# Factors of batch 1 turned with batch 0's, three more stores on GpSimd, and the last chunk copied and stored in halves

## The chip, the cores and the metric

The kernel runs on one core of a Trainium2 chip. PE is TensorE (matrix products), DVE is VectorE, ACT is ScalarE, POOL is GpSimd, SP is SyncE, which only issues transfers. Each engine works through its own instructions in order and waits for the others by semaphores. The metric is the device time of one execution in microseconds; less is better.

## The reference

A chunked state space scan (4 batches, 8 heads, 768 steps, head width 32, state 16), and a GELU layer on its result:

```python
log_a = np.log(np.clip(a, 1e-06, 1.0))
for c in range(nc):                       # chunks of 32
    cum = np.cumsum(la, axis=-1)
    L = np.exp(cum[:, :, :, None] - cum[:, :, None, :]) * causal
    y_intra = einsum('bhij,bhjd->bhid', einsum('bhin,bhjn->bhij', Cc, Bc) * L, xc)
    y_inter = einsum('bhin,bhnd->bhid', Cc, state) * exp(cum)[..., None]
    y[:, :, sl] = y_intra + y_inter
    state = decay_full * state + sum_j(Bc x xc * decay_from_j)
x = y.transpose(0, 2, 1, 3).reshape(3072, 256)
out = gelu_tanh(x @ w_in) @ w_out         # 256 -> 2048 -> 256
```

## The kernel before

**Tiling.** The kernel uses chunks of 128 steps: 24 chunks `gc`, in 12 pairs `j` or `u` of 256 steps. Batch b holds pairs 3b to 3b+2, so pairs 0 to 2 are batch 0, and 3 to 5 batch 1. The first five pairs (`j < TOK`, TOK = 5) hold their steps in another order in memory, even and odd steps apart, than the later ones.

**Factors.** Decay is applied by scaling B with running products R of `a`, and C with 1/R. `f_clip` and `f_R` make R for all batches at once (`r_t`, 96 rows: part, batch, head). PE turns it so that steps lie on partitions: a product with `r_t` as the weights and the selection matrix `sel` as the moving operand, in fp32 (helper `rt_mm`, line 310). `f_RT` does this at the start for batch 0: two products of 24 columns, `rps[0]` in the PSUM bank pair `gb0`. DVE takes reciprocals (`f_rc0`, `f_rc1`), ACT copies R (`f_rlo`), and both stand in the tile `fac0`. `f_RTN` does it later, near 17 us: two products of 96 columns for all batches in the later order, and four of 8 columns for pairs 3 and 4, which have the earlier order. ACT copies this to `fac` (`f_rn`), and DVE takes reciprocals batch by batch (`f_pn`). `f_mul(j, i)` multiplies C (i = 1) or B (i = 0) of a pair with its factors.

**One pair.** After `f_mul`, B and C are transposed (on PE, `f_T`, for pairs 0 to 3, by a DMA issued on SP for later ones) and copied by ACT (`bt`). DVE masks heads (`f_F`, `ce`). PE then forms the Gram products `f_G` (L467 or L456, into `gb`), which DVE masks (`f_M`, tile `m`). `f_D` (L576 or L564) forms B times x for the state; DVE makes the running state from it (`f_S`, `s_new`; `f_SP`, `sp_new`). `f_Y` and `f_I` form y, and `xm` is its copy in bf16. x is cast to bf16 by GpSimd (`f_castx`).

**The layer.** For each pair, 32 matmuls `f_s1` (L642) fill four PSUM banks `bk` by turns, in eight groups of four, and ACT applies the GELU (`f_gelu`, tile `gT`, L650). Then 16 matmuls `f_s2` (L659) for each chunk; the result is copied out of PSUM (`f_oev`, tile `o_sb`; ACT, but DVE for chunks 21 and 23) and stored (`f_store`). Chunks 0 to 15 (`NPS = 16`) are stored by GpSimd's queue, and 16 to 23 by SP's. The pool of `o_sb` has six buffers.

**What sets the order.** The kernel builds a list of nodes with an engine, an estimated duration, dependencies and a priority. `run_order` plays them through, engine by engine, and the instructions are issued in the order that comes out; each engine then keeps that order. `FIRST` lists the first loads after `HEAD`, all issued on SP. The waits themselves are put in by the tile framework from what each instruction reads and writes.

Of the kernel before, what the change touches and what calls it, by code (L numbers as in the profile page):

```python
# [8 lines left out]
FP32 = mybir.dt.float32  # L9
# [104 lines left out]
def kernel(  # L114
# [10 lines left out]
    nc = tc.nc  # L125
# [3 lines left out]
    Q = 128  # L129
# [9 lines left out]
    TOK = 5  # L139
# [117 lines left out]
    pm = const.tile([128, 4 * D], BF16, name="pm")  # L257
    pp0 = const.tile([128, 4], FP32, name="pp0")
    r_t = const.tile([RA, W], FP32, name="r_t")
    fac0 = const.tile([128, 2, T3, 2, H], FP32, name="fac0")  # L260
    fac = const.tile([128, 2, batch, T3, 2, H], FP32, name="fac")
    pend = const.tile([128, NCH], FP32, name="pend")
    rps = {}
# [8 lines left out]

    X16 = {}
    state = {}
    gts, ops, hps = {}, {}, {}


    wo = moe_w_out.rearrange("(k f) m -> f k m", f=128)
# [32 lines left out]
                         start=True, stop=True, skip_group_check=True)  # L311

    def f_RT():
        rps[0] = GB[0][:, 0, 0:2 * T3 * H].rearrange("p (r t h) -> p t r h", r=2, t=T3)
        for r in range(2):
            rt_mm(GB[0][:, 0, r * T3 * H:(r + 1) * T3 * H],
                  r_t.rearrange("q (p r) -> q r p", r=2)[:, r], sel[:, :, 0:H])

    def f_RTN(bk):
        rps["n"] = bk[:, 0:NCH * H].rearrange("p (r i b h) -> p r b i h", r=2, i=T3, b=batch)  # L320
        for r in range(2):
            rt_mm(bk[:, r * RA:(r + 1) * RA], r_t[:, r * Q:(r + 1) * Q],
                  sel.rearrange("p i j -> p (i j)"))
        for j in range(T3, TOK):
            b, t = divmod(j, T3)
            for r in range(2):
                o = r * RA + (t * batch + b) * H
                rt_mm(bk[:, o:o + H], r_t.rearrange("q (p r) -> q r p", r=2)[:, r], sel[:, t, b * H:(b + 1) * H])

    def f_rc0():  # L330
        nc.vector.reciprocal(fac0[:, 1, 0], rps[0][:, 0])

    def f_rc1():
        nc.vector.reciprocal(fac0[:, 1, 1:T3], fac0[:, 0, 1:T3])

    def f_rlo():
        nc.scalar.activation(fac0[:, 0], rps[0], AF.Copy)

    def f_rn(r):
        nc.scalar.activation(fac[:, 0, :, :, r], rps["n"][:, r], AF.Copy)  # L340

    def f_pn(b):
        nc.vector.reciprocal(fac[:, 1, b], fac[:, 0, b])
# [36 lines left out]
    def f_mul(j, i):  # L380
        d = P[j]
        b, t = divmod(j, T3)
        if "bc16" not in d:
            d["bc16"] = work.tile([128, 2, 2, H, N], BF16, name="bc16")
        f = fac[:, i, b, t] if b else fac0[:, i, t]
        nc.vector.tensor_tensor(  # L386
            out=d["bc16"][:, i], in0=d["bc"][:, i].rearrange("p h (r n) -> p r h n", r=2) if j < TOK else
            d["bc"][:, i].rearrange("p h m -> p (h m)").rearrange("p (r h n) -> p r h n", r=2, h=H),
            in1=f.rearrange("p r (h o) -> p r h o", o=1).to_broadcast([128, 2, H, N]), op=ALU.mult)
# [264 lines left out]
    def f_s2(g, tt, q, bk=None):  # L654
# [3 lines left out]
        for fi in range(4 * q, 4 * q + 4):  # L658
            nc.tensor.matmul(out=ops[gc], lhsT=gts[g][:, fi, tt * Q:(tt + 1) * Q],  # L659
                             rhs=w_out_sb[:, fi, :], start=(fi == 0), stop=(fi == NF - 1),  # L660
                             skip_group_check=True)

    def f_oev(gc, eng):
        o_sb = opool.tile([128, d_model], FP32, name="o_sb")
        if eng == "ACT":
            nc.scalar.activation(o_sb, ops.pop(gc), AF.Copy)  # L666
        else:
            nc.vector.tensor_copy(out=o_sb, in_=ops.pop(gc))  # L668
        ops[gc] = o_sb
# [14 lines left out]
    DF = 1.0  # L684
    DW = 1.0
    LANES = 8
    FIRST = [("c", 3), ("b", 3), ("x", 3)]
    NPS = 16
    PET = {0: "ACT", 1: "ACT", 2: "ACT", 3: "ACT"}
    LB, LX, LI, LO, XD, XL = 0.92, 1.25, 1.42, 1.5, 0.6, 3.6  # L690
    HEAD = [("x", 0), ("x", 1), ("b", 1), ("wi", 1), ("wi", 2), ("wi", 3), ("b", 2), ("wo", 0), ("wo", 1), ("c", 2), ("wo", 2), ("wo", 3), ("x", 2)]
# [120 lines left out]
    frees(RTN, *rnn)  # L812
    pnn = {b: add("DVE", 0.42, f_pn, b, deps=rnn, prio=100 + b) for b in range(1, batch)}

    def gone(j):
        return [Yn.get(j - WB)]

    trn = add("POOL", 0.9, f_trk, deps=[wo_n[3][-1]], prio=25)
    for j in range(NP):
# [2 lines left out]
        b, t = divmod(j, T3)  # L822
        if b and t == 0:
            pnn[b].deps += Mn[j - (1 if j in PET else XA)]
        hold = Mn.get(j - (AHEAD if j in PET else XA), [])
        pj = PP if j == 1 else p
        ml = {i: shared(add("DVE", 0.43, f_mul, j, i, done=0.08, prio=pj - 0.1 * i if j else -179 - i,
                            deps=[bl[j, i], *hold, pnn[b] if b else rlo if not i else rc1 if j else rc0, *gone(j)]))
              for i in (1, 0)}
        bnn[j] = ml[0]  # L830
        if j == 1:
# [108 lines left out]
    for g, (c0, n) in enumerate(GROUPS):  # L940
        per = 512 // (n * Q)
        ends_ = []
        for tt in range(n):
            gc = c0 + tt
            if g < TWO and tt:
                prev = ahead
            ahead = list(prev)
            for q in range(4):
                need = [geln[(g, i)] for i in range(4 * n) if i * per <= 4 * q + 3]
                nd = add("PE", 0.437, f_s2, g, tt, q, deps=need[-1:] + wo_n[q] + prev,  # L950
                         prio=PB + 10 * c0 + 10 * n + 2.5 * ((tt + 2 * q) if g < TWO else 4 * tt + q) + 1.2,
                         alloc="bk" if q == 0 else ())
                if q == 0:
                    first = nd
                prev = [nd]
            ends_.append(nd)
            oeng = "DVE" if gc >= NCH - TAIL and gc % 2 else "ACT"
            oevn[gc] = add(oeng, 0.4, f_oev, gc, oeng, deps=[nd], prio=-40)
            frees(first, oevn[gc])
            if g < TWO:  # L960
                prev = list(ends_)
            if gc < NPS:
                st_n = add("POOL", 1.1, f_store, gc, nc.gpsimd, deps=[oevn[gc]], prio=2000)
            else:
                add("OUT", 0.05, f_store, gc, nc.sync, deps=[oevn[gc]], prio=gc)
# [65 lines left out]
```

## Time and profile before

| | us |
|---|---|
| median of 3 runs | 117.15 |
| the runs | 117.15, 116.15, 117.15 |
| the profiled execution's own time | 116.17 |
| its span | 114.5 |
| busy in it: PE / ACT / DVE / POOL | 107.7 / 72.8 / 59.6 / 30.1 |

The span is from the first to the last instruction that the profiler saw; the execution's own time also holds what lies around it. Busy times are summed for each engine over the span. Rows of the timeline begin with start and duration in us; `x4` is a count; in brackets stands the idle time of the engine just before, and what ended it. PE runs many matmuls overlapped, and PEld is its weight load. An fp32 product leaves two records.

### The profile page before, as it was taken

Reading aid. Unit: us, or ns where it says so; the run is one execution under the profiler, and the core shown is the slowest. Engines: PE = TensorE matmul, PEld = TensorE weight load, DVE = VectorE, ACT = ScalarE, POOL = GpSimd, SP = SyncE. Lnnn points to the kernel's source line nnn. Section 1 sums busy time; section 2 is a strip of 40 time slices with the busy share of each in tenths; the row PEclk is TensorE's granted clock in tenths of the full one; section 3 lists DMA queues with packets and bytes.
Section 4 is the critical chain, followed back from the end, with each engine's and each line's share of the span. In section 5 each row is a group of like instructions: output and inputs, shape, how many; then the busy total and the mean of one; then the engine's idle time right before and its main releaser. Section 6 shows DMA issues by size and latency. Waiting matters only on the chain.

```text
span 114.5 us, 3620 instructions
## 1 busy us (share of the span) xinstructions
PE 107.7 (94%) x1505; PEld 88.1 (77%) x1505; DVE 59.6 (52%) x133; ACT 72.8 (64%) x160; POOL 30.1 (26%) x57
## 2 busy tenths in 40 slices
PE   5987989999999999999999999999999999999970
PEld 2553669878878788887887887888878878878850
DVE  2799994069569293850952925907909227000110
ACT  0557685971469377686684793865966857949510
POOL 6834765746410421104211401412110000000000
PEclk9999999999999999999999999999999999999999
DMA  3999999999789897599977869674122011011021
GB/s 61 261 266 388 342 326 305 195 190 187 130 156 125 70 184 119 78 142 88 161 111 133 151 83 161 98 108 105 46 46 95 3 46 49 6 46 46 2 90 46
DMA packets 68880, 15.01 MB, mean 131 GB/s; under 512 B 64160, under 2 KB 67328, under 8 KB 68864
## 3 DMA queue, kind: packets, MB, share of 16 engines
q1 hardware_dynamic: 63888, 10.20, 53.3%
q10 hardware_dynamic: 4208, 2.49, 7.2%
q0 software_dynamic: 768, 2.10, 4.9%
q8 instruction: 11, 0.18, 0.7%
q14 instruction: 5, 0.04, 0.1%
HBM read 10.58 MB, written 3.15 MB: 120 GB/s over the span
## 4 chain that ended last, share of the span: by engine, by line
PE 85%; DVE 6%; ACT 4%; issue 2%; DVEq 0%
PE bk L659 37%; PE bk L642 33%; PE gb L993 4%; PE bk L526 2%; DVE sp_new L625 2%; PE gb L456 1%; ACT gT L650 1%; PE bk L310 1%; PE bk L500 1%; ACT bt L287 1%; DVE ce L432 1%; PE bk L549 1%; PE gb L467 1%; ACT sp_new L620 1%; PE gb L310 1%
## 5 line engine op out<-in xcount | busy, mean ns | idle before, releaser
L650 ACT ACTIVATE gT<-bk 128x512 bf16<-128x512 f32 x96 | 50.3, 604 | 7.6 <-PE bk L642 7.4
L659 PE MATMUL bk<-w_out_sb,gT 128*128 128x256 bf16 x384 | 48.7, 273 | 0.0
L642 PE MATMUL bk<-xm,w_in_sb 128*128 128x256 bf16 x384 | 47.2, 273 | 0.3 <-DVE s_new L609 0.3
L659 PEld LDWEIGHTS <-gT 128*128 128x128 bf16 x384 | 36.6, 98 | 6.1 <-issue 1.8
L642 PEld LDWEIGHTS <-w_in_sb 128*128 128x128 bf16 x384 | 37.3, 98 | 5.1 <-issue 0.6
L674 POOL DMA_DIRECT2D out_dram<-o_sb x16 | 8.9, 554 | 44.0 <-ACT o_sb L666 42.0
L477 DVE TENSOR_TENSOR m<-gb,trk 128x1024 bf16<-128x1024 f32 x14 | 17.0, 1216 | 0.0
L666 ACT ACTIVATE o_sb<-bk 128x256 f32<-128x256 f32 x22 | 8.5, 386 | 12.1 <-PE bk L659 6.0
L609 DVE SCALAR_TENSOR_TENSOR s_new<-s_new,pend,bk 128x64 f32<-128x64 f32 x16 | 4.4, 274 | 18.8 <-ACT xm L287 18.7
L287 ACT ACTIVATE xm<-bk 128x256 bf16<-128x256 f32 x22 | 7.4, 381 | 9.2 <-PE bk L500 6.9
L386 DVE TENSOR_TENSOR bc<-bc,fac 128x256 bf16<-128x256 f32 x24 | 10.9, 480 | 1.1 <-DMA bc<-in_C_dram 1.0
L477 DVE TENSOR_TENSOR m<-gb,tri 128x1024 bf16<-128x1024 f32 x8 | 9.6, 1216 | 0.2 <-PE gb L467 0.2
L289 POOL CAST x<-x_t 128x512 bf16<-128x512 f32 x12 | 7.5, 628 | 5.8 <-DMA x_t<-in_x_dram 5.7
L432 DVE TENSOR_SCALAR ce<-bt,par 128x256 bf16<-128x256 bf16 x22 | 5.6, 294 | 5.8 <-ACT bt L287 5.7
L625 DVE SCALAR_TENSOR_TENSOR sp_new<-s_new,pend,pm 128x128 bf16<-128x128 f32 x19 | 8.3, 464 | 0.0
L668 DVE COPY o_sb<-bk 128x256 f32<-128x256 f32 x2 | 0.8, 424 | 14.0 <-PE bk L659 14.0
L993 PE MATMUL gb<-wz 128*128 128x512 bf16 (+2 forms) x17 | 5.7, 465 | 1.3 <-DVE warm L221 1.3
L993 PEld LDWEIGHTS <-wz 128*128 128x128 bf16 x25 | 2.9, 127 | 3.9 <-issue 2.2
L607 DVE COPY s_new<-bk 128x64 f32<-128x64 f32 x3 | 0.7, 225 | 8.5 <-ACT xm L287 7.7
L289 POOL CAST w_in_sb<-wf 128x1024 bf16<-128x1024 f32 x4 | 4.6, 1157 | 1.6 <-DMA wf<-in_moe_w_in_dram 1.6
L289 POOL CAST w_out_sb<-wf 128x1024 bf16<-128x1024 f32 (+1 forms) x4 | 3.8, 940 | 2.5 <-DMA wf<-in_moe_w_out_dram 2.5
L456 PE MATMUL gb<-ce,bt 32*64 32x256 bf16 x112 | 3.3, 274 | 0.0
(78 smaller groups left out, 58.4 us busy)
## 6 DMA issues: line engine op xcount, KB each, us to landing
wf<-in_moe_w_in_dram ACTq DMA_DIRECT2D x4, 512.0 KB, 7.8
wf<-in_moe_w_out_dram SPq DMA_DIRECT2D x4, 512.0 KB, 6.7
out_dram<-o_sb POOLq DMA_DIRECT2D x16, 128.0 KB, 2.7
x_t<-in_x_dram SPq DMA_DIRECT2D x14, 128.0 KB, 3.3
x_t<-in_x_dram SPq DMA_DIRECT2D x5, 256.0 KB, 5.7
out_dram<-o_sb SPq DMA_DIRECT2D x8, 128.0 KB, 1.7
bc<-in_C_dram SPq DMA_DIRECT2D x14, 64.0 KB, 3.4
bc<-in_B_dram SPq DMA_DIRECT2D x14, 64.0 KB, 3.4
```

The lines of the kernel that those rows point to most:

```text
L287: nc.scalar.activation(o, i, AF.Copy)
L289: nc.gpsimd.tensor_copy(out=o, in_=i)
L386: nc.vector.tensor_tensor(out=d["bc16"][:, i], in0=d["bc"][:, i].rearrange("p h (r n) -> p r h n", r=2) if j < TOK else d["bc"][:, i].rear ...
L432: nc.vector.tensor_scalar(out=d["ce"][:, e], in0=v, scalar1=par[:, e:e + 1], scalar2=None, op0=ALU.mult)
L477: nc.vector.tensor_tensor(out=state[("m", u, f)].rearrange("p g r e t -> p g (r e t)"), in0=state.pop(("gc", u, f), gram[f]).rearrange("p ...
L625: nc.vector.scalar_tensor_tensor(out=sp_new.rearrange("p (j d) -> p j d", j=2), in0=state[("s", gc)].rearrange("p (o d) -> p o d", o=1).to ...
L642: nc.tensor.matmul(out=hp[:, j * nt:(j + 1) * nt], lhsT=w_in_sb[:, kc, fi * 128:(fi + 1) * 128], rhs=xm[:, kc, c0 * Q:c0 * Q + nt], start= ...
L650: nc.scalar.activation(gts[g][:, i * per:(i + 1) * per, 0:nt], hps.pop((g, i)).rearrange("p (j t) -> p j t", j=per), AF.Gelu_apprx_tanh)
L659: nc.tensor.matmul(out=ops[gc], lhsT=gts[g][:, fi, tt * Q:(tt + 1) * Q], rhs=w_out_sb[:, fi, :], start=(fi == 0), stop=(fi == NF - 1), ski ...
L666: nc.scalar.activation(o_sb, ops.pop(gc), AF.Copy)
L674: q.dma_start(out=o.rearrange("(p r) m -> r p m", r=2)[r] if u < TOK else o[r * Q:(r + 1) * Q], in_=ops.pop(gc))
L993: nc.tensor.matmul(out=bank[:, 0:128 * w], lhsT=wz[:, 0:128], rhs=wz[:, 0:128 * w], start=True, stop=True)
```

## The change

Four things are changed.

- `f_RT` takes 16 columns of `sel` for each part instead of 8, so 48 columns in each product instead of 24: batches 0 and 1. `fac0` becomes twice as wide. The reciprocals of batch 0 and the copy on ACT go with it, and a new node `f_p3` on DVE takes the reciprocals of batch 1 for pairs 3 and 4. `f_RTN` loses its four 8-column products. `f_mul` takes the factors of all pairs below TOK from `fac0`.
- `FIRST` has another order of loads (C of pair 4 ahead of x of pair 3).
- `NPS` is 19 instead of 16: chunks 16 to 18 are stored by GpSimd's queue.
- The last chunk's output is copied in two halves of 128 columns, one on ACT and one on DVE, and each half is stored by a queue of its own, ACT's and SP's.

```diff
-    fac0 = const.tile([128, 2, T3, 2, H], FP32, name="fac0")
+    fac0 = const.tile([128, 2, T3, 2, 2 * H], FP32, name="fac0")
...
     def f_RT():
-        rps[0] = GB[0][:, 0, 0:2 * T3 * H].rearrange("p (r t h) -> p t r h", r=2, t=T3)
+        n = T3 * 2 * H
+        rps[0] = GB[0][:, 0, 0:2 * n].rearrange("p (r t c) -> p t r c", r=2, t=T3)
         for r in range(2):
-            rt_mm(GB[0][:, 0, r * T3 * H:(r + 1) * T3 * H],
-                  r_t.rearrange("q (p r) -> q r p", r=2)[:, r], sel[:, :, 0:H])
+            rt_mm(GB[0][:, 0, r * n:(r + 1) * n], r_t.rearrange("q (p r) -> q r p", r=2)[:, r], sel[:, :, 0:2 * H])
...
-        for j in range(T3, TOK):
-            b, t = divmod(j, T3)
-            for r in range(2):
-                o = r * RA + (t * batch + b) * H
-                rt_mm(bk[:, o:o + H], r_t.rearrange("q (p r) -> q r p", r=2)[:, r], sel[:, t, b * H:(b + 1) * H])
 
     def f_rc0():
-        nc.vector.reciprocal(fac0[:, 1, 0], rps[0][:, 0])
+        nc.vector.reciprocal(fac0[:, 1, 0, :, 0:H], rps[0][:, 0, :, 0:H])
 
     def f_rc1():
-        nc.vector.reciprocal(fac0[:, 1, 1:T3], fac0[:, 0, 1:T3])
+        nc.vector.reciprocal(fac0[:, 1, 1:T3, :, 0:H], fac0[:, 0, 1:T3, :, 0:H])
...
+    def f_p3():
+        nc.vector.reciprocal(fac0[:, 1, 0:TOK - T3, :, H:2 * H], fac0[:, 0, 0:TOK - T3, :, H:2 * H])
...
-        f = fac[:, i, b, t] if b else fac0[:, i, t]
+        f = fac[:, i, b, t] if j >= TOK else fac0[:, i, t, :, b * H:(b + 1) * H]
...
+    def f_oevs(gc, h, eng):
+        hs = slice(h * 128, h * 128 + 128)
+        o_sb = opool.tile([128, 128], FP32, name="o_half")
+        copy(eng, o_sb, ops[gc][:, hs])
+        halves[h] = o_sb
+
+    def f_half(gc, h, q):
+        u, r = divmod(gc, 2)
+        hs = slice(h * 128, h * 128 + 128)
+        q.dma_start(out=out[u * W + r * Q:u * W + (r + 1) * Q, hs], in_=halves[h])
...
-    FIRST = [("c", 3), ("b", 3), ("x", 3)]
-    NPS = 16
+    FIRST = [("c", 3), ("b", 3), ("c", 4), ("x", 3), ("b", 4), ("x", 4)]
+    NPS = 19
...
+    p3n = add("DVE", 0.15, f_p3, deps=[rlo], prio=100)
...
+        if j == T3:
+            p3n.deps += Mn[1]
...
-                            deps=[bl[j, i], *hold, pnn[b] if b else rlo if not i else rc1 if j else rc0, *gone(j)]))
+                            deps=[bl[j, i], *hold, pnn[b] if j >= TOK else p3n if j >= T3 else rlo if not i else rc1 if j else rc0, *gone(j)]))
...
-            oevn[gc] = add(oeng, 0.4, f_oev, gc, oeng, deps=[nd], prio=-40)
+            if gc == NCH - 1:
+                ev2 = [add(e, 0.25, f_oevs, gc, h, e, deps=[nd], prio=-40 + h) for h, e in enumerate(("ACT", "DVE"))]
+                frees(first, *ev2)
+                s0 = add("ACT", 0.1, f_half, gc, 0, nc.scalar, deps=[ev2[0]], prio=-39)
+                add("OUT", 0.05, f_half, gc, 1, nc.sync, deps=[ev2[1], s0], prio=gc)
+                continue
+            else:
+                oevn[gc] = add(oeng, 0.4, f_oev, gc, oeng, deps=[nd], prio=-40)
```

Lines below the changed places carry other numbers in the changed program (L642 becomes L640, L659 becomes L657, L467 becomes L465, L576 becomes L574).

The first place is PE near 17 us, where `f_RTN` stands between the products of the second pair's y (L512, L510) and the layer's next matmuls. Before:

```order
L512 LDWEIGHTS sp_new_422
L512 MATMUL bk2_161<-bt_278,sp_new_422 64x128
L310 MATMUL bk3_162<-sel_114,r_t_150 128x96 x2
L310 MATMUL bk3_162<-sel_114,r_t_150 128x8 x4
L642 LDWEIGHTS w_in_sb_154
L642 MATMUL bk1_160<-xm_156,w_in_sb_154 128x256
```

Now:

```order
L510 LDWEIGHTS sp_new_422
L510 MATMUL bk2_161<-bt_278,sp_new_422 64x128
L310 MATMUL bk3_162<-sel_114,r_t_150 128x96 x2
L640 LDWEIGHTS w_in_sb_154
L640 MATMUL bk1_160<-xm_156,w_in_sb_154 128x256
```

The four products of 8 columns are gone, and what stands around them is as it was. On DVE, `f_p3` now stands ahead of the multiply of B of pair 2, which precedes the copy of half of `xm` of pair 1; the reciprocals of `f_pn(1)` move behind the multiplies of pair 3.

The second place is PE at pair 3, where `f_D` (operand `x16`, the cast x) and `f_G` (operands `ce` and `bt`) of that pair begin. Before, `f_D` came straight ahead of `f_G`, and 32 matmuls L642 followed. Now `f_G`, four L640, `f_D`, eight L657 and the other 28 L640 follow one another. This is the end of `f_G`, and the seam from the four L640 to `f_D`:

```order
L465 MATMUL gb1_158<-ce_719,bt_668 64x256
L640 LDWEIGHTS w_in_sb_154
L640 MATMUL bk3_162<-xm_156,w_in_sb_154 128x256
L574 LDWEIGHTS bc16_630
L574 MATMUL bk2_161<-x16_714,bc16_630 32x64
```

The rows that repeat are left out. `f_D` has moved from ahead of `f_G` to behind the four matmuls that follow it. GpSimd's cast of x of pair 3 has moved too, from behind its first store to behind its second. The eight L657 ahead of the 28 L640 stood ahead of the transposes of pair 3 before, where twelve of them went; four of the twelve stand just behind those transposes now.

The third place is the end of the program: the last two copies on DVE, and the last on ACT, with the semaphores that they wait for (`PE_49` is raised by PE, `Activation_49` by ACT, and the names with DMA by stores that have landed). Before, on DVE and then on ACT:

```order
L668 COPY o_sb_2207<-bk0_159 128x256 [waits DMASW3_49,DMASW7_49,DMASW1_49,PE_49]
L668 COPY o_sb_2241<-bk2_161 128x256 [waits DMASW5_49,DMASW3_49,DMAHW3_49,PE_49,Activation_49]
L1026 UNCONDITIONAL_BRANCH
L650 ACTIVATE gT_2149<-bk1_160 128x512 [waits PE_49]
L666 ACTIVATE o_sb_2226<-bk3_162 128x256 [waits DMAHW2_49,PE_49,Activation_49]
```

Now, in the same order:

```order
L677 COPY o_sb_2204<-bk1_160 128x256 [waits DMASW3_49,DMASW7_49,DMASW1_49,PE_49]
L291 COPY o_half_2240<-bk2_161 128x128 [waits Activation_49]
L1046 UNCONDITIONAL_BRANCH
L675 ACTIVATE o_sb_2223<-bk3_162 128x256 [waits DMASW0_49,PE_49,Activation_49]
L287 ACTIVATE o_half_2238<-bk2_161 128x128 [waits PE_49]
L670 DMA out_0_dram<-o_half_2238 128x128 [waits DMAHW6_49,Activation_49]
```

Both halves read the bank `bk2`; ACT's waits for PE, and DVE's for ACT alone.

2 lines of the change are left out of this document (1 added, 1 removed).

## The prediction

> **What bounds the kernel now.** I read the table of busy times by stretches first, then the chain of work that ended last, then the timeline at the places which the change touches.
>
> ```profile
> core 0: us, PE busy (x) PEld busy (x) DVE busy (x) ACT busy (x) POOL busy (x), PEclk, DMA share, GB/s
> 24.90:110.95 86.05, 85.99 (x1218) 72.99 (x1210) 43.28 (x92) 56.80 (x123) 14.53 (x25) 1.00 0.59 97
> 17.00:24.90 7.90, 7.83 (x89) 6.89 (x85) 2.35 (x5) 6.44 (x14) 5.15 (x7) 1.00 1.00 238
> 0.00:17.00 17.00, 13.93 (x212) 8.25 (x212) 13.52 (x35) 9.57 (x23) 10.42 (x26) 1.00 1.00 273
> ```
>
> Columns are the stretch, its length, then each engine's busy time. From 17.00 us on PE (TensorE) is busy 7.83 of 7.90 us and then 85.99 of 86.05 us: it is the bound, and work taken from it comes off the end unless a wait takes its place. Before 17 us PE has gaps and a chain through DVE and ACT sets the pace. After 110.95 PE is done and a tail follows. The chain agrees:
>
> ```profile
> 17.07 1.49 PE bk L310 x12
> 18.55 2.20 PE bk L642 x20
> ...
> 106.96 3.94 PE bk L659 x36
> ...
> 110.98 0.42 DVE o_sb L668
> ```
>
> Twelve fp32 records of line 310 (the products that turn the decay factors, `f_RTN`) stand on it for 1.49 us. The tail is the last chunk's copy by DVE, then its store.
>
> **The products for batch 1 (removed).** f_RTN loses its four 8-column products. Each product leaves two records (six instructions, twelve records), so eight records go.
>
> ```profile
> 17.00 1.55 PE L310 MATMUL bk<-sel,r_t 96*128 96x96 f32 x12
> 17.59 0.97 PE L310 MATMUL bk<-sel,r_t 96*128 96x8 f32 x7
> 18.41 2.34 PE L642 MATMUL bk<-xm,w_in_sb 128*128 128x256 bf16 x20
> ```
>
> The second row is the last seven of the eight small records: from 17.59 to the start of the next matmul at 18.41 is 0.82 us, 0.117 us each; eight are 0.94 us. Is PE really free to go on? What follows are four L642 matmuls of the first chunk pair, whose inputs are long ready, and then those of the second pair, which need `xm`:
>
> ```profile
> 17.22 0.42 DVE L291 CAST xm<-bk 128x256 bf16<-128x256 f32 x1 [0.31 <-PE bk L512]
> L334 DVE RECIPROCAL fac<-fac 128x32 f32<-128x32 f32 x1 | 0.3, 341 | 0.0
> ```
>
> The new reciprocal `f_p3` stands on DVE ahead of the multiply before that xm copy. It has as many elements as L334, so 0.34 us, and DVE has 0.31 us idle before its half of xm: that half ends near 17.67 instead of 17.64. PE needs it after the four matmuls: the four wide records take 17.00 + 4 x 0.117 = 17.47, and four L642 at 0.11 each (2.20/20 in the chain) make it 17.91. So the reciprocal costs nothing here; without that 0.24 us cover it would cost up to 0.34. Next come ACT and the weights:
>
> ```profile
> 19.04 4.19 ACT L650 ACTIVATE gT<-bk 128x512 bf16<-128x512 f32 x8
> 20.02 1.04 POOL L289 CAST w_out_sb<-wf 128x1024 bf16<-128x1024 f32 x1 [0.75 <-DMA wf<-in_moe_w_out_dram]
> 18.61 0.93 DVE L386 TENSOR_TENSOR bc<-bc,fac 128x256 bf16<-128x256 f32 x1 [0.97 <-DMA bc<-in_C_dram]
> 22.77 0.39 PE L408 MATMUL bk<-ident,bc 128*128 128x128 bf16 x4
> 23.87 0.60 PE L659 MATMUL bk<-w_out_sb,gT 128*128 128x256 bf16 x4
> ```
>
> ACT's eight gelus start when PE's first group and the copies of the L310 result are done; both move with PE. What cannot move are the transfers: the third quarter of w_out is cast at 21.06, its matmuls would come at 23.87 - 0.94 = 22.93; the multiply that waited for C ends at 19.54, its transposes would come at 21.83. Both have over 1.8 us left. So I take the whole 0.94. The other end is a wait that eats 0.34 of it (first rival).
>
> **The same products for batch 0 (doubled in width, on the early chain).**
>
> ```profile
> 1.25 3.49 PE L993 MATMUL gb<-wz 128*128 128x512 bf16 x9 [1.25 <-DVE warm L221]
> 4.53 0.99 PE L310 MATMUL gb<-sel,r_t 96*128 96x24 f32 x4
> 8.60 1.14 PE L993 MATMUL bk<-wz 128*128 128x512 bf16 x5
> L331 DVE RECIPROCAL fac<-gb 128x16 f32<-128x16 f32 x1 | 0.3, 258 | 0.6 <-PE gb L310 0.6
> ```
>
> DVE sits idle for them (0.6 us, last row), so an increase here counts. They go from 24 to 48 columns. Above, at 17 us, 96-column and 8-column records follow each other at the same 0.117 us, so width up to 96 hides behind the weight load: lower end 0. At 4.5 us PE runs at about half speed (0.39 us per 512-column matmul in the first row against 0.23 in the third). If a column cost all it could, 0.117/96 = 1.2 ns, doubled for the speed, 24 columns x 4 records give 0.23 us: upper end. I take 0.05, near the lower end, because only the last record's drain cannot hide. [...] The later ACT copy of 96 instead of 48 elements runs beside a DVE multiply.
>
> **Order of work around chunk pair 3.** The planner puts that pair's state products `f_D` (L576) between L642 and L659, where they stood next to its `f_G` (L467).
>
> ```profile
> 24.53 0.42 PE gb L467 x16
> ...
> 31.99 0.18 PE bk L576 x16
> 32.17 0.35 PE gb L467 x16
> ```
>
> G alone costs 0.42 (first row), after D 0.35; so splitting costs 0.07 plus perhaps as much for D between large matmuls: 0.1, bounds 0 to 0.2. D now also waits for the cast of x of pair 3, whose load is issued one place later (c4 first) and whose cast stands behind GpSimd's second store.
>
> ```profile
> 21.58 0.75 SPq L198 DMA_DIRECT2D x_t<-in_x_dram  x1
> DMA to landing us min/median/max: 3.8/3.9/4.0
> 27.98 0.55 POOL L674 DMA_DIRECT2D out_dram<-o_sb  x1 [0.37 <-ACT o_sb L666]
> ```
>
> (The middle row is of the x loads between 20 and 30 us.) Load: 21.58 + one C issue of about 0.6 + 4.0 = 26.2. Cast: behind the second store, 27.98 - 0.9 + 0.55 = 27.6, plus 0.63 = 28.3. D is due about 31.0 (31.99, less 0.94, less eight L659 that now come later, plus G's 0.42 and four L642). No wait, unless a load took over 6.
>
> **Three more stores on GpSimd (NPS).** Chunks 16 to 18 leave SP's queue for GpSimd's. Behind them GpSimd has no cast left; on SP no load or transpose stands behind them. The output buffers come round six chunks later, far beyond any landing. Cost 0.
>
> **The last chunk.** Read as parallel halves, DVE's 0.42 us copy becomes 0.3 us on each of two engines. But ACT and DVE read one PSUM bank, and the code's other place of that kind shows what happens:
>
> ```profile
> L337 ACT ACTIVATE fac<-gb 128x48 f32<-128x48 f32 x1 | 0.2, 211 | 1.4 <-DVE fac L331 1.4
> L606 ACT ACTIVATE s_new<-bk 128x64 f32<-128x64 f32 x1 | 0.3, 257 | 0.0
> L666 ACT ACTIVATE o_sb<-bk 128x256 f32<-128x256 f32 x22 | 8.5, 386 | 12.1 <-PE bk L659 6.0 <-ACT xm L287 4.5 <-issue 1.6
> L607 DVE COPY s_new<-bk 128x64 f32<-128x64 f32 x3 | 0.7, 225 | 8.5 <-ACT xm L287 7.7 <-PE bk L576 0.7
> L668 DVE COPY o_sb<-bk 128x256 f32<-128x256 f32 x2 | 0.8, 424 | 14.0 <-PE bk L659 14.0
> ```
>
> L337 and L331 both read `gb`, and ACT was released by DVE, not by PE. In the changed program DVE's half waits for ACT's in the same way. So: ACT from about 110.97 for 0.30 (a third of the way from 64 to 256 columns, 257 to 386), then DVE for 0.29 (225 to 424): 111.59, where it was 111.40. That is +0.19. [...] Copies side by side would end at 111.27, 0.13 earlier than now.
>
> ```profile
> 112.20:112.60 0.40, 0.00 (x0) 0.00 (x0) 0.00 (x0) 0.00 (x0) 0.00 (x0) 1.00 0.79 274
> DMA to landing us min/median/max: 1.7/1.7/3.1
> ```
>
> The first row is a stretch inside the last store's flight (its 0.79 is the DMA share), the second is of SP's eight stores. The last store lands 1.7 us after its issue, about 0.3 of it moving data (0.79 of that 0.40); a half can save 0 to 0.2, I take 0.1. ACT's half, issued near 111.3, lands before. Tail: +0.1, bounds -0.3 (copies side by side, all of the 0.2 saved) to +0.2.
>
> **Sum.** The profiled execution took 116.17 us (span 114.5). -0.94 + 0.05 + 0.10 + 0.10 = -0.69, so 115.5 for it. The runs shown lie at 116.15 and 117.15 (twice), with the profiled one at the lower level. Against the median, 117.15 - 0.69 = **116.4**, 0.6% faster. About 1% is what a measurement here tells from no change.
>
> **Rivals.** *A wait replaces the products:* xm's DVE half comes late because the reciprocal is slower than L334 or waits. For it: DVE has only 0.31 idle there. Against: the 0.24 us of cover. Price up to 0.34: 116.8. Chance 0.13.
>
> *The larger gain:* early products cost 0, no switch cost, store cheaper: 117.15 - 0.94 - 0.1 = 116.1. If in addition the changed kernel's median falls on the lower of the two levels, 115.1 to 115.5. Two of four executions shown lie there. Chance that the measured time is over 1% lower, by this or by the level alone: 0.30.
>
> *Slower: the half store on ACT's queue becomes the last thing.* Place: after 111.3 us. All 24 stores, GpSimd's among them:
>
> ```profile
> DMA to landing us min/median/max: 1.7/2.6/4.4
> ```
>
> If ACT's landed after 3.1 (SP's worst) it would end at 114.4 instead of 113.1, +1.3 on a kernel that gained 0.79 elsewhere: 117.7; after 4.4, 119.0. It decides against the change from 113.1 + 0.8 = 113.9 on, a landing of 2.6 us. For it: ACT issues no store now, and GpSimd's take longer than SP's. Against: SP's median is its minimum, 1.7, and the queues are idle there. Chance 0.10, 0.06 of it over 1%.
>
> *The change does not do what it says* is in the sum already: the halves are not side by side.
>
> **Chances.** Forecast 0.47, wait 0.13, lower level or larger gain 0.30, slower 0.10. Faster by over 1% 0.30; within 1% the forecast, the wait and 0.04 of the slower case, 0.64; slower 0.06. Range 115.2 to 117.3.
>
> **What would show it.** L310 with 8 records instead of 16, L642 following at about 17.6 instead of 18.41, and that 0.9 us lead kept in the chain to the end of PE near 110.2. The fac0 reciprocal at 5.6, not later than 5.65. At the end DVE's half released by ACT, not PE. If L642 still starts after 18, or PE idles before D of pair 3, or the landing of ACT's half ends the run, I am wrong.

## The result, and the profile after

The changed kernel takes 115.66 us (median of 20 runs, 114.49 to 117.01), the kernel before 116.34 us (20 runs beside it, 115.29 to 118.14). The ratio is 0.9933, with a 95% interval of 0.9908 to 0.9959: 0.7% faster. Ratios here and below compare fast executions alone (those over 1.5% above the fastest of their kernel are left out), so they are not the quotient of the medians. The forecast of 116.4 started from the median of the three runs shown, 117.15; its difference of -0.69 us, taken from 116.34, gives 115.65. The difference was right in size, the level 0.7 us too high. Whether the difference was made of the terms that were named is what the traces and the experiments have to tell. The profiled execution took 115.72 us (span 114.0; before 116.17 and 114.5).

First the table of stretches, with the cuts at the start of the late turn of factors (`f_RTN`), behind the second pair's Gram products, and at PE's end. The columns are those of the prediction's first table.

```profile
core 0: us, PE busy (x) PEld busy (x) DVE busy (x) ACT busy (x) POOL busy (x), PEclk, DMA share, GB/s
0.00:16.57 16.57, 13.56 (x211) 7.68 (x211) 12.43 (x35) 9.61 (x23) 8.70 (x24) 1.00 0.97 271
16.57:24.15 7.58, 7.08 (x80) 5.94 (x77) 2.84 (x6) 6.44 (x14) 4.41 (x5) 1.00 0.73 201
24.15:110.90 86.75, 86.12 (x1218) 72.89 (x1210) 43.45 (x93) 56.82 (x123) 19.13 (x32) 1.00 0.58 102
```

The middle stretch, where before had 0.07 us of idle PE, now has 0.50, and the last one 0.63 where before had 0.06. PE's end is where it was (110.90; before 110.89). PE's timeline shows the two places, and GpSimd's what it waited for:

```profile
16.57 0.69 PE L310 MATMUL bk<-sel,r_t 96*128 96x96 f32 x4
17.75 2.36 PE L640 MATMUL bk<-xm,w_in_sb 128*128 128x256 bf16 x20 [0.49 <-POOL w_in_sb L289]
...
23.76 0.42 PE L465 MATMUL gb<-ce,bt 32*64 32x256 bf16 x16
24.80 1.36 PE L657 MATMUL bk<-w_out_sb,gT 128*128 128x256 bf16 x11 [0.62 <-POOL w_out_sb L289]
```

```profile
16.66 1.04 POOL L289 CAST w_in_sb<-wf 128x1024 bf16<-128x1024 f32 x1 [1.93 <-DMA wf<-in_moe_w_in_dram]
...
23.88 0.87 POOL L289 CAST w_out_sb<-wf 128x512 bf16<-128x512 f32 x1 [1.23 <-DMA wf<-in_moe_w_out_dram]
```

The same two casts before, in GpSimd's timeline:

```profile
14.85 1.31 POOL L289 CAST w_in_sb<-wf 128x1024 bf16<-128x1024 f32 x1 [0.49 <-DMA wf<-in_moe_w_in_dram]
...
21.86 0.61 POOL L289 CAST w_out_sb<-wf 128x512 bf16<-128x512 f32 x1 [0.80 <-DMA wf<-in_moe_w_out_dram]
```

In this execution the last quarters of both weights came 1.8 and 2.0 us later than in the profiled execution of before, and the chain of waits now runs through them:

```profile
14.06 7.50 DMA wf<-in_moe_w_out_dram
21.62 1.04 POOL w_out_sb L289
22.65 1.21 issue
23.89 0.87 POOL w_out_sb L289
24.80 2.78 PE bk L657 x24
...
106.97 3.94 PE bk L657 x36
```

So the second pair's Gram products start 0.77 us earlier (23.76 against 24.53), and all of it is lost at 24.80. DVE's timeline has the first reciprocal of the early factors, and PE's the seam at pair 3:

```profile
5.34 0.26 DVE L326 RECIPROCAL fac<-gb 128x16 f32<-128x16 f32 x1 [0.34 <-PE gb L310]
```

```profile
30.95 0.42 PE L465 MATMUL gb<-ce,bt 32*64 32x256 bf16 x16
31.30 0.61 PE L640 MATMUL bk<-xm,w_in_sb 128*128 128x256 bf16 x4
31.84 0.25 PE L574 MATMUL bk<-x,bc 64*32 64x64 bf16 x16
32.03 1.05 PE L657 MATMUL bk<-w_out_sb,gT 128*128 128x256 bf16 x8
```

No wait stands ahead of D (L574). The end of the run in the timeline, and then what SP waited for after its half store (total, times, longest):

```profile
110.93 0.28 ACT L287 ACTIVATE o_half<-bk 128x128 f32<-128x128 f32 x1 [1.31 <-PE bk L657]
111.24 0.37 ACTq L670 DMA_DIRECT2D out_dram<-o_half  x1
111.24 0.29 DVE L291 COPY o_half<-bk 128x128 f32<-128x128 f32 x1 [3.38 <-ACT o_half L287]
111.56 0.33 SPq L670 DMA_DIRECT2D out_dram<-o_half  x1
```

```profile
SPq L1046 <- DMA out_dram<-o_half: 0.7, 2, 0.5
```

The halves are serial, as forecast: DVE's was released by ACT's. The last copy ends at 111.53 (before 111.41), the last landing is at 113.11 (before 113.13). The span is nonetheless 0.45 us shorter: what follows the last landing takes 0.90 us instead of 1.34. That is nearly the whole gain of these two executions, at a place which the prediction did not look at.

What stands there is SP's list of closing waits, eight of them on the semaphores of the hardware queues' DMAs, in a fixed order of names (100, 102, 103, 105, 106, 107, 108, 110). SP's records of the two traces, with the time left to the end of the span in ns, and the first semaphore that each waits for; the last store's semaphore is marked:

```
before                               after
 -3031 last store raises 102          -2450 SP's half raises 110 (ACT's 108)
 -2584 wait 100                       -2013 wait 100
 -1319 wait 102   <- last store       -1952 wait 102
 -1255 wait 103                       -1888 wait 103
 -1193 wait 105                       -1826 wait 105
 -1134 wait 106                       -1767 wait 106
 -1072 wait 107                       -1705 wait 107
 -1013 wait 108                       -1181 wait 108   <- ACT's half
  -951 wait 110                        -882 wait 110   <- SP's half
  -886 drain                           -817 drain
```

Each wait costs SP some 62 ns even when its semaphore has long been raised. Before, six stood behind the one that came last, some 0.37 us; now none does, since the other seven are done while the store flies. (The other 0.07 of the 0.44 us lies in the records after the list; e3, e5 and e6, which have six waits behind too, take 1.27 or 1.28.) In both traces the semaphores are dealt out in turn to the DMAs of SP and ACT, so the place of the last store's is set by how many DMAs the hardware queues have issued: three stores fewer on SP (NPS) and one half store more on ACT move it.

### The profile page after: what moved, and what is told of

The parts are those of the page before. It is cut to its first block, busy times and chain, and to the rows that moved or that the text cites. A ratio compares the mean times of both kernels' runs of the same rounds, so it can differ in the third digit from the quotient of the medians.

```text
span 114.0 us, 3606 instructions
## 1 busy us (share of the span) xinstructions
PE 106.8 (94%) x1497; PEld 86.5 (76%) x1497; DVE 59.0 (52%) x134; ACT 73.1 (64%) x161; POOL 32.2 (28%) x60
## 3 DMA queue, kind: packets, MB, share of 16 engines
HBM read 10.58 MB, written 3.15 MB: 120 GB/s over the span
## 4 chain that ended last, share of the span: by engine, by line
PE 76%; DMA 11%; SPq 5%; POOL 3%; issue 2%; ACTq 1%; DVE 0%; ACT 0%; POOLq 0%
PE bk L657 37%; PE bk L640 31%; DMA wf<-in_moe_w_out_dram 7%; DMA wf<-in_moe_w_in_dram 5%; SPq L283 3%; PE bk L524 2%; POOL w_out_sb L289 2%; PE gb L454 2%; SPq L183 1%; PE bk L498 1%; ACTq L183 1%; POOL w_in_sb L289 1%; PE bk L547 1%; PE gb L465 1%; PE bk L510 0%
## 5 line engine op out<-in xcount | busy, mean ns | idle before, releaser
L657 PE MATMUL bk<-w_out_sb,gT 128*128 128x256 bf16 x384 | 49.1, 273 | 0.6 <-POOL w_out_sb L289 0.6
L640 PE MATMUL bk<-xm,w_in_sb 128*128 128x256 bf16 x384 | 47.5, 273 | 0.8 <-POOL w_in_sb L289 0.8
L640 PEld LDWEIGHTS <-w_in_sb 128*128 128x128 bf16 x384 | 37.0, 98 | 6.1 <-POOL w_in_sb L289 1.5
L657 PEld LDWEIGHTS <-gT 128*128 128x128 bf16 x384 | 36.5, 98 | 6.7 <-issue 2.4
L683 POOL DMA_DIRECT2D out_dram<-o_sb x19 | 10.5, 553 | 45.4 <-ACT o_sb L675 45.4
L289 POOL CAST x<-x_t 128x512 bf16<-128x512 f32 x12 | 8.3, 690 | 10.6 <-DMA x_t<-in_x_dram 10.6
L623 DVE SCALAR_TENSOR_TENSOR sp_new<-s_new,pend,pm 128x128 bf16<-128x128 f32 x19 | 7.4, 420 | 0.1
L287 ACT ACTIVATE bt<-bk 128x256 bf16<-128x256 bf16 (+1 forms) x5 | 2.4, 473 | 1.7 <-PE bk L406 1.7
```

The costliest lines, as they stand in the source:

```text
L287: nc.scalar.activation(o, i, AF.Copy)
L289: nc.gpsimd.tensor_copy(out=o, in_=i)
L623: nc.vector.scalar_tensor_tensor(out=sp_new.rearrange("p (j d) -> p j d", j=2), in0=state[("s", gc)].rearrange("p (o d) -> p o d", o=1).to ...
L640: nc.tensor.matmul(out=hp[:, j * nt:(j + 1) * nt], lhsT=w_in_sb[:, kc, fi * 128:(fi + 1) * 128], rhs=xm[:, kc, c0 * Q:c0 * Q + nt], start= ...
L683: q.dma_start(out=o.rearrange("(p r) m -> r p m", r=2)[r] if u < TOK else o[r * Q:(r + 1) * Q], in_=ops.pop(gc))
```

## The experiments

Five theories. **A**: the terms of the prediction hold. **B**: the halves make the gain in the tail. **C**: the place of the last store's semaphore in the closing list makes it. **D**: transfers of weights take part of PE's lead. **E** (formed after the first runs): DVE's masking of C for the second pair (`ce`) is slowed by what GpSimd does beside it, and PE waits for it.

All runs were timed beside the kernel before, on the same chip (e5 to e8 on another chip than the rest). Changes in us are the ratio's distance from 1 times 116.5, the level of before in these comparisons.

### The parts, one at a time

*e1_tail: the kernel before with the two halves alone.*

```diff
-            oevn[gc] = add(oeng, 0.4, f_oev, gc, oeng, deps=[nd], prio=-40)
+            if gc == NCH - 1:
+                ev2 = [add(e, 0.25, f_oevs, gc, h, e, deps=[nd], prio=-40 + h) for h, e in enumerate(("ACT", "DVE"))]
...
```

> The kernel before with the last chunk in halves alone. From the prediction (A): the copies end 0.12 to 0.19 us later, the half store flies 0.1 to 0.14 us shorter, so the time is the same within 0.1 us, ratio 1.000 to 1.001. If the halves themselves make the shorter end of the changed kernel (B): 0.45 us less between PE's end and the end of the span, ratio 0.996. If the end is set by where the last store's semaphore stands in SP's closing list of waits (C): here it stands one place later than before, so from the last landing to the end about 1.34 - 0.06 = 1.28 us, and ratio 0.999 to 1.000.

*e2_nps: the kernel before with three more stores on GpSimd.*

```diff
-    NPS = 16
+    NPS = 19
```

> The kernel before with three more stores on GpSimd alone. By the prediction (A) this costs and gains nothing: ratio 1.000, from the last landing to the end 1.34 us as before. By the place of the last store's semaphore in SP's closing list (C): three fewer stores on the hardware queues put the last one five places later in that list, 0.062 us each, so 1.34 - 0.31 = 1.03 us from the last landing to the end, and ratio 0.997.

*e3_factors: the factors of batch 1 turned with batch 0's, nothing else (old order of first loads, NPS 16, no halves; the planner puts G ahead of D at pair 3 here too).*

```diff
-            rt_mm(GB[0][:, 0, r * T3 * H:(r + 1) * T3 * H],
-                  r_t.rearrange("q (p r) -> q r p", r=2)[:, r], sel[:, :, 0:H])
+            rt_mm(GB[0][:, 0, r * n:(r + 1) * n], r_t.rearrange("q (p r) -> q r p", r=2)[:, r], sel[:, :, 0:2 * H])
...
-        for j in range(T3, TOK):
...
```

> The kernel before with the factors of batch 1 alone. By the prediction (A) PE is free to use the 0.94 us: 0.8 to 0.9 us less, ratio 0.992 to 0.993, and PE ends 0.8 us earlier than before. If the transfers of the two weights set the front as soon as PE gets ahead (D): PE is ahead by some 0.8 us near 23 us and loses most of it waiting for casts of w_in and w_out, 0.2 to 0.3 us less in all, ratio 0.997 to 0.998.

*e4_after: the changed kernel again.* No edit.

> The changed kernel again, for its time on this chip and for a second execution's trace. Ratio 0.993 by the first measurement. If its first trace was typical (C and D), PE waits again for casts of w_in or w_out between 17 and 25 us, and 0.9 us lie between the last landing and the end. If that wait was one execution's accident (A), PE ends near 110.1 and the span is near 113.2.

Measured: e1 0.9946 (0.9904 to 0.9988), e2 0.9946 (0.9908 to 0.9983), e3 0.9945 (0.9905 to 0.9985), e4 0.9916 (0.9877 to 0.9955). Each part alone brings some 0.6 us with half a microsecond of uncertainty, so the times alone cannot rank them. The traces can, place by place:

| us | before | e1 | e2 | e3 | after | e4 |
|---|---|---|---|---|---|---|
| start of the late turn | 17.00 | 17.03 | 17.22 | 17.50 | 16.57 | 17.54 |
| from it to the layer's next matmul | 1.41 | 1.41 | 1.41 | 0.52 | 1.18 | 0.52 |
| second pair's Gram products | 24.53 | 24.95 | 24.91 | 24.54 | 23.76 | 24.30 |
| PE's idle time just ahead of them | 0.07 | 0.45 | 0.22 | 0.46 | none | 0.17 |
| PE's end | 110.89 | 111.31 | 111.27 | 111.09 | 110.90 | 110.76 |
| last landing | 113.13 | 113.52 | 113.52 | 113.31 | 113.11 | 112.97 |
| landing to end | 1.34 | 1.20 | 0.96 | 1.28 | 0.90 | 0.90 |

The last row is theory C's. e2, which changes no copy and no size of the last store, has 0.96; its last store raises semaphore 108, with one wait behind it. e1 has the halves and 1.20 (semaphore 103, five waits behind). The halves themselves come to nothing: from PE's end to the last landing it is 2.24 us before and 2.22 in e1 and in the changed kernel, and 2.22 in e3 too, which has no halves. SP's drains, which follow the list, show it: e2's last landing is at 113.52 and the first drain at 113.7, where before has 113.13 and 113.6. The records of e2, then of before (durations in ns, first and last start):

```profile
L1026 SPq DRAIN  x3: 7/7/7, 113.7 to 114.0; - x3
```

```profile
L1026 SPq DRAIN  x3: 7/7/7, 113.6 to 113.9; - x3
```

### One store instead of three

*e9_nps17: the kernel before with one store more on GpSimd.* By theory C this must bring nothing, since the semaphore moves to the list's first place (100).

```diff
-    NPS = 16
+    NPS = 17
```

> The kernel before with NPS 17, one store more on GpSimd's queue instead of three. The last store's semaphore then stands one place earlier in the closing list than in the kernel before (eighth from the end... that is, seven more waits behind it, where there are six in the kernel before and two with NPS 19). Theory C (place in the list): 1.30 to 1.40 us from the last landing to the end, ratio to before 1.000 (within 0.002). The rival, that fewer stores on SP's queue are what saves time: a third of what NPS 19 brought (0.9946), ratio 0.998, and about 1.15 from landing to end.

Measured: 1.0002 (0.9968 to 1.0036), and 1.33 us from the landing at 113.07 to the end, with seven waits behind the last store's. (With NPS 19 one wait stands behind it, not two: e2's store raises 108, and only 110 follows.) SP's wait for that store stands first, and longer than in e2, whose seven others were done while the store flew; e9's row, then e2's:

```profile
SPq L1026 <- DMA out_dram<-o_sb: 1.3, 1, 1.3
```

```profile
SPq L1026 <- DMA out_dram<-o_sb: 0.9, 1, 0.9
```

One store moved gives +0.02 us, three give -0.63. The interval of this time still holds the rival's 0.998; the trace decides, with 1.33 us from landing to end where the rival had 1.15. What follows the last landing is not set by the load on SP's queue.

### The changed kernel without the halves

*e7_nps18: chunk 18 stays on SP's queue, and the last chunk is one copy and one store, whose semaphore is 110, last in the list.*

```diff
-    NPS = 19
+    NPS = 18
...
-            if gc == NCH - 1:
...
+            oevn[gc] = add(oeng, 0.4, f_oev, gc, oeng, deps=[nd], prio=-40)
```

> The changed kernel without the halves: the last chunk is copied out by DVE alone and stored by SP alone; chunks 16 and 17 go to GpSimd's queue, chunk 18 stays on SP's, so that the last store's semaphore stands last in the closing list, as SP's half does in the changed kernel. Theory C (the place of the semaphore in the list makes the tail's gain): 0.90 us from the last landing to the end, about 3.12 from PE's end to the end of the span against 3.11 in the changed kernel, ratio 0.992 to 0.993, equal to the changed kernel within 0.1 us. Theory B (the halves bring the tail's gain): 0.2 to 0.4 us slower than the changed kernel, ratio 0.995 or more.

Measured: 0.9934 (0.9900 to 0.9968); 0.92 us from landing to end, 3.14 from PE's end to the end of the span (3.12 in the changed kernel). Without the halves nothing is missing. Theory C is shown for what follows the last landing, and B falls for the tail. The times of e1 and e2 stay partly open: from landing to end they gain 0.14 and 0.37 us in the traces, 0.63 by their ratios, where C had 0.12 or less for e1 and 0.35 for e2; e1's interval only begins at 0.14.

### The removed records, less and more

*e5_minus* leaves out the four small products; *e6_plus* issues them twice. The order of everything else is before's.

```diff
-        for j in range(T3, TOK):
-            b, t = divmod(j, T3)
-            for r in range(2):
...
```

```diff
-        for j in range(T3, TOK):
+        for j in [*range(T3, TOK)] * 2:
```

> The kernel before, with the four products of 8 columns of the late turn of factors left out and the order of everything else kept; the factors of chunk pairs 3 and 4 are then those of the later order, so these pairs are computed with other numbers, and no work but those eight records is missing. Theory A (the removed records count in full): the late turn takes about 0.5 us from its start to the layer's next matmul instead of 1.41, PE ends 0.94 earlier relative to the start of the turn, 115.8 beside a before of 116.75, ratio 0.992. Theory D (the loads of w_in's and w_out's last quarters, and other work of that stage, set PE's pace there, so that part of the lead is given back): the stage itself shortens by 0.9, but PE then waits 0.4 to 0.6 us for a cast or for DVE's masked C; PE ends 0.3 to 0.5 earlier, ratio 0.996. The tail is that of before: 1.2 to 1.35 from the last landing to the end.

> The kernel before, with the four products of 8 columns of the late turn done twice, so eight records more; the order of everything else is kept. Theory A: 0.94 more, about 2.35 us from the turn's start to the layer's next matmul, ratio 1.008 (117.7 beside 116.75). Theory D: what PE waits for weights or masked C in before disappears under the added records, so less is added, 0.6 or so, ratio 1.005. A and D differ in whether e5's saving and this cost are of one size (A) or the saving is clearly smaller than the cost (D).

Measured: e5 0.9929 (0.9890 to 0.9968), -0.83 us; e6 1.0044 (1.0001 to 1.0088), +0.51 us. At the place itself the records count in full: 0.52 us from the turn's start to the next matmul in e5, 1.41 in before, 2.35 in e6. Further down PE's timeline, first e5's, then e6's:

```profile
17.04 0.69 PE L310 MATMUL bk<-sel,r_t 96*128 96x96 f32 x4
17.56 2.35 PE L637 MATMUL bk<-xm,w_in_sb 128*128 128x256 bf16 x20
...
24.27 0.42 PE L462 MATMUL gb<-ce,bt 32*64 32x256 bf16 x16 [0.64 <-DVE ce L427]
```

```profile
17.31 2.50 PE L310 MATMUL bk<-sel,r_t 96*128 96x96 f32 x20
19.66 2.34 PE L642 MATMUL bk<-xm,w_in_sb 128*128 128x256 bf16 x20
...
25.93 0.32 PE L467 MATMUL gb<-ce,bt 32*64 32x256 bf16 x8 [0.21 <-DVE ce L432]
```

Half the distance between the two runs is 0.67 us per eight records, about 0.34 either way; A's 0.94 is inside, D's 0.3 to 0.5 as well. By the times the saving is not smaller than the cost, which spoke for A against D. The traces say otherwise. From the turn's start to PE's end it is 93.89 us before, 93.58 in e5 and 94.98 in e6: 0.31 saved, 1.09 added. PE's work changes by what A says (0.89 less, 0.94 more, when its idle time is taken off), but PE idles 0.07, 0.64 and 0.21 us of it, all ahead of the second pair's Gram products. So e5 gives most of its lead back, as D had it (0.3 to 0.5 left), and not to a weight: to `ce`, which D named as the other possibility and theory E would explain. This is one trace each. DVE's row and GpSimd's beside it, in e5:

```profile
22.98 1.23 DVE L427 TENSOR_SCALAR ce<-bt,par 128x256 bf16<-128x256 bf16 x2 [2.66 <-ACT bt L287]
...
22.99 0.61 POOL L289 CAST w_out_sb<-wf 128x512 bf16<-128x512 f32 x1 [1.17 <-DMA wf<-in_moe_w_out_dram]
23.54 0.53 POOL L439 MEMSET trk<- 128x512 bf16 x1
```

Both GpSimd's cast of w_out's last quarter and the mask stand beside the masking here. Over all fourteen traces the two DVE instructions take 0.48 us where GpSimd does nothing beside them (e10 and the changed kernel's first trace), and 0.62 to 1.45 in the twelve others, where it casts w_out or x, or makes its mask `trk`.

### The late mask on GpSimd made early

*e8_trk: the changed kernel with GpSimd's mask `trk` (memset and affine selects) made at the start, and e10_trk the same again beside e11_after, the changed kernel.*

```diff
-    trn = add("POOL", 0.9, f_trk, deps=[wo_n[3][-1]], prio=25)
+    trn = add("POOL", 0.9, f_trk, deps=[pen], prio=-99)
```

> The changed kernel with GpSimd's making of the late mask (a memset and the affine selects, which stood at about 22 to 24 us beside DVE's masking of C for the second pair's Gram products) moved to the start of GpSimd's work. Theory E (GpSimd's writes and DVE's masking slow each other): DVE's two masking instructions take 0.48 us each in every execution, and PE does not wait for them ahead of the second pair's Gram products; 0.1 to 0.4 us faster than the changed kernel, ratio to before 0.989 to 0.991. Theory A or D: no change beside the changed kernel, ratio 0.992 to 0.993; if the early mask delays the first casts, it is slower.

> The kernel of e8 once more (the changed kernel with GpSimd's late mask made at the start), now beside the changed kernel on the same chip. Theory E: DVE's masking of C for the second pair takes 0.7 us or less for both instructions and PE does not wait for it; 0.1 to 0.3 us below e11. Rival: e8's lead came from an early landing of weights and an early warm PE alone, then equal to e11 within 0.1 us.

> The changed kernel once more, as the measure for e10 and e12. Ratio to before 0.992 to 0.993; 0.90 us from the last landing to the end; PE's end 110.7 to 110.9 in the profiled execution.

Measured: e8 0.9910 (0.9877 to 0.9944), e10 0.9886 (0.9829 to 0.9944), e11 0.9868 (0.9810 to 0.9926). In the traces of e10 and e8 PE does not wait for `ce`, or hardly (none and 0.07 us). The masking and the products that follow it, in e10 and then, with GpSimd's cast beside it, in e11:

```profile
22.73 0.48 DVE L430 TENSOR_SCALAR ce<-bt,par 128x256 bf16<-128x256 bf16 x2 [3.88 <-ACT bt L287]
...
23.30 0.42 PE L465 MATMUL gb<-ce,bt 32*64 32x256 bf16 x16
```

```profile
22.37 1.12 DVE L430 TENSOR_SCALAR ce<-bt,par 128x256 bf16<-128x256 bf16 x2 [2.18 <-ACT bt L287]
...
22.27 0.61 POOL L289 CAST w_out_sb<-wf 128x512 bf16<-128x512 f32 x1 [0.44 <-DMA wf<-in_moe_w_out_dram]
...
23.55 0.42 PE L465 MATMUL gb<-ce,bt 32*64 32x256 bf16 x16 [0.53 <-DVE ce L430]
```

e10's PE ends at 109.76 and e8's at 110.15, the first and the third earliest of all fourteen traces here, with e11's 110.01 between them. From the turn's start to PE's end they take 92.97 (e10) and 93.11 us (e8), 0.92 and 0.78 less than before: where PE waits for nothing on the way, the lead arrives. But it is not shown that the early mask took the wait away. The cast of w_out's last quarter, which ran beside the masking in e11, had also ended before it in e10 and e8 (21.27 and 22.47); and in e8 a cast of x beside it still made it 0.66 us, where E expected 0.48 in every execution (0.48 is the time of the two together, not of each). The times do not follow either: E had e10 below e11 by 0.1 to 0.3 us, and it is not below (six runs each, medians 115.77 and 115.34), and e8 is below e7 by 0.0024 with wide intervals. No version here is shown to beat the changed kernel.

### One weight transfer less

*e12_wo3: the changed kernel with 4 KB loaded in place of w_out's last quarter.*

```diff
-            WF[("o", q)] = wfp.tile([128, 4, d_model], FP32, name="wf")
-        e.dma_start(out=WF[("o", q)], in_=wo[:, 4 * q:4 * q + 4])
+            WF[("o", q)] = wfp.tile([128, 4, d_model], FP32, name="wf") if q < 3 else WF[("o", 2)]
+        e.dma_start(out=WF[("o", q)] if q < 3 else const.tile([128, 8], FP32, name="small"), in_=wo[:, 4 * q:4 * q + 4] if q < 3 else wo[:, 12, 0:8])
```

> The changed kernel without the load of w_out's last quarter (512 KB): a load of 4 KB takes its place, and the casts of that quarter read the third quarter's tile, so the layer is computed with the third quarter twice; all instructions and their order are kept. Theory D (late transfers of weights take part of the lead): PE does not wait for a cast of w_out, later transfers land earlier, 0.2 to 0.4 us below e11. Theory E (the masking of C beside GpSimd's mask is what PE waits for): the mask on GpSimd follows that cast and moves forward with it; PE's wait ahead of the second pair's Gram products stays or changes by chance, within 0.1 us of e11.

Measured: 0.9963 (0.9933 to 0.9992), above e11 by 1.1 us by the ratios and by 0.6 by the medians (115.93 and 115.34). Both theories missed. With less to load, the third quarter came later, and PE waited for that:

```profile
22.71 1.59 POOL L289 CAST w_out_sb<-wf 128x1024 bf16<-128x1024 f32 x2 [1.59 <-DMA wf<-in_moe_w_out_dram]
...
23.80 0.60 PE L657 MATMUL bk<-w_out_sb,gT 128*128 128x256 bf16 x4 [0.66 <-POOL w_out_sb L289]
```

The lag is there before the edit's place: the transfers between 8 and 10 us moved 226 GB/s in this trace and 344 in e11's. The first row is e12's, the second (in the next fence) e11's:

```profile
8.00:10.00 2.00, 1.13 (x30) 0.78 (x24) 2.00 (x3) 1.81 (x7) 1.62 (x3) 1.00 1.35 226
```

```profile
8.00:10.00 2.00, 1.27 (x20) 0.67 (x28) 1.81 (x3) 1.98 (x7) 0.80 (x2) 1.00 1.09 344
```

Why is open. The trace shows that a late w_out costs PE time, and the run does not show what one transfer less would be worth.

## Why the prediction was right in size, point by point

**-0.94 for the removed records ("So I take the whole 0.94").** At its place it was right: 0.52 instead of 1.41 us, -0.89. On the way to PE's end it was mis-sized, and the sign named for it failed: PE's end was to come near 110.2, and came at 110.90, 110.76 and 110.01 in the changed kernel's three traces. (The other sign, the layer's next matmul at about 17.6, hangs on when the turn begins: it came at 17.75, 18.06 and 16.94.) The step looked at the third quarter of w_out and at C, and said both had over 1.8 us left. What came late was neither: the last quarter of w_in and of w_out in the first trace of the changed kernel (0.49 and 0.62 us), w_in's again in e11 (0.18), and `ce` in e3, e4, e7 and e11 (0.46, 0.17, 0.27, 0.53). The chain of waits of before had said where to look: it leaves PE ahead of the second pair's Gram products.

```profile
21.66 1.57 ACT gT L650 x3
23.24 0.57 ACT bt L287
23.80 0.02 issue
23.83 0.67 DVE ce L432 x2
24.49 0.04 issue
```

Here `ce` ended as PE's earlier work did, so any growth of it is PE's loss. The runs give 0.67 +- 0.34 (e5 and e6); PE's end, as a mean of five traces with the change of factors (the changed kernel's three, e3, e7) against four without (before, e1, e2, e9), gives 0.33, with the +0.10 of the split of D and G in it. How much of the lead arrives differs from execution to execution. The wait that replaces the products was a rival, but its place was wrong: `xm` was never late.

**+0.05 for the wider early products.** From the first weight load of the early turn to DVE's reciprocal it is 1.14 us in before and e9 and 1.09 in e2 (24 columns), and 1.17 and 1.18 in e3 and e10 and 1.13 in e4 and e12 (48): +0.04 where the load began at the same time (4.43, or about 4.5). In before, e2, e3 and e4 PE was slow there: the three matmuls of 512 columns behind the turn took 1.01, 1.04, 1.27 and 1.27 us. Where the turn itself was quicker, the two widths are alike: 0.72 and 0.73 in e6 and e5, 0.71 to 0.73 in e7, e8 and e11 (in e11 the three matmuls took 0.71). So the 5.34 at which the reciprocal began in the changed kernel's first trace (5.57 before) is not the change, but a PE that sped up earlier: the three matmuls took 0.71 us there and 1.01 in before, and 0.70 in e1, which has 24 columns. The width hides almost wholly: 0.04 of the 0.23 us that the prediction had as its upper end. That the last record's drain is what cannot hide was the author's estimate; no run isolates it.

**+0.10 for the split of D and G at pair 3.** From the second pair's Gram products to PE's end it is 86.36 us in before and in e9, 86.46 in e4, e8, e10 and e11: +0.10, with no wait for the cast of x. e3 and e7, which have G ahead of D too, take 86.55 and 86.64, so the cost is 0.10 to 0.28; why it differs is open.

**0 for NPS.** This step failed. It asked who would be late on either queue, found nobody, and did not ask what the end of the program waits for. By the closing list NPS alone takes five of the six waits away, 0.31 us (0.96 in e2 against 1.27 in e5 and e6), and the half store on ACT's queue, one DMA more, takes the sixth: 0.37 for the two. e2's time says 0.63 with 0.20 to 1.07 possible, and e9's trace says that the number of stores is not the cause.

**+0.10 for the tail.** Serial copies cost +0.12 (forecast +0.19), the smaller store saved 0.14 (forecast 0.1): about nothing. ACT's half landed before SP's, as the order of the closing waits shows, so the slower rival fell.

**The sum by what was measured**: -0.67 + 0.04 + 0.10 - 0.02 for the halves - 0.37 for the list = -0.92. The changed kernel was measured three times: -0.78, -0.98 and -1.54 us, which weighted by the inverse squares of their intervals is -0.92, about 0.23 either way. That the two agree so closely is chance, since the first term alone is uncertain by 0.34. The forecast of -0.69 came out near in part by luck: a gain taken too large (by about 0.27) and one not seen at all (0.37), with the tail's 0.1, lean opposite ways.

**What stays open**: why weights land up to 2 us apart in executions whose first part is the same program (w_in's last cast began at 14.85 in before and at 17.15 in e1), why the late turn begins anywhere from 16.07 to 17.54 us, how much of the 0.89 us reaches the end on average, and why e12 is slower.

## What to carry to other kernels

Ask of a gain on the bounding engine not only whether the next input is early, but what the chain of waits passed through a little later: a node that ended just in time before can be the next bound (here `ce`: PE idled 0.07 us ahead of the products that need it in before, and 0.17 to 0.53 in e3, e4, e7 and e11). Look past the last landing: the closing waits are part of the time, and what moves the last transfer's semaphore (a count of earlier transfers, not their work) was worth more here (0.37 us) than what was done to the transfer (0.02). Where one change has several parts, time each alone and read each at its own place in the trace, since a total near the forecast can hide two errors.

## What the runs showed of the hardware that was not expected

- SP's closing waits take about 0.062 us each, even when their semaphores have long been raised (the lists of before and of the changed kernel's first trace, above). With seven waits behind the last store's semaphore (e9), six (before, e3, e5, e6), five (e1), one (e2) and none (the changed kernel, e4, e7), landing to end took 1.33, 1.27 to 1.34, 1.20, 0.96 and 0.90 to 0.92 us.
- DVE's two masking instructions take 0.48 us together where GpSimd does nothing beside them (e10, and the changed kernel's first trace), 0.66 beside a cast of x (e8), 1.23 beside a cast of w_out and then the memset (e5), and 1.45 beside its casts in e12 (row below). No run here isolates the cause.

```profile
22.93 1.45 DVE L430 TENSOR_SCALAR ce<-bt,par 128x256 bf16<-128x256 bf16 x2 [1.52 <-ACT bt L287]
```

- PE speeds up at different times from execution to execution, though its first matmul starts at 1.25 or 1.26 in before, e3, e11 and the changed kernel's first trace. The three matmuls of 512 columns behind the early turn took 0.71 us in the changed kernel's first trace, 1.01 in before and 1.27 in e3 (rows of the first and the last below, in this order). In e11 the nine ahead of the turn, which end at 4.41, already took 3.15 us, against 3.49 in those three; in e3 two matmuls of 128 columns (L400) still took 0.42 us at 6.64, against 0.28 in e11. So PE sped up more than 2 us later in e3 than in e11. The late turn does not follow this alone: it began at 16.79, 16.98 and 17.54 in e10, e12 and e4, where ACT's copy of the early factors began within 0.02 us (5.90 to 5.92).

```profile
5.14 0.71 PE L1013 MATMUL gb<-wz 128*128 128x512 bf16 x3
```

```profile
5.37 1.27 PE L1006 MATMUL gb<-wz 128*128 128x512 bf16 x3
```
